# Batch 0 of a Fourier and channel-mix kernel: mirrored rows turned by a copy and added by TensorE, x by plain loads

## The chip, the core and the metric

The kernel runs on one NeuronCore of a Trainium2 chip. Its engines work side by side, each through its own instructions in order: TensorE (PE in the profile, its weight loads PEld), VectorE (DVE), ScalarE (ACT), GpSimd (POOL) and SyncE (SP). TensorE multiplies a stationary operand, loaded first, with a moving one, and writes to PSUM; the others evacuate PSUM to SBUF. Transfers are issued from the queues of SP, ACT and POOL. The metric is the device time of one execution, in microseconds; lower is better.

## The reference

```python
x = randn(8, 3072, 256) * 0.1                       # batch, seq, dim
X = np.fft.fft(np.fft.fft(x, axis=1), axis=2).real   # 2-D Fourier transform, real part
x_prev = X shifted by one row along seq, zero first
xk = mu_k * X + (1 - mu_k) * x_prev
xr = mu_r * X + (1 - mu_r) * x_prev
k = np.maximum(xk @ w_k, 0)                          # 256 -> 1024
v = k * k @ w_v                                      # 1024 -> 256
out = v / (1 + np.exp(-(xr @ w_r)))
```

## The kernel before, in words

The real part of the 2-D transform is a sum of cosines, and row s, column d gives the same as row -s, column -d. So each row of x is added to its mirrored row, read backwards, before anything is multiplied: `fold` (L160 to L175) writes p = x + mirrored x with two VectorE instructions for a piece of rows, one for all columns and one that puts column 0 right. That halves the first stage.

The sequence is taken apart as 3072 = 48 x 64. Batch 0 and 1 lie on 96 partitions (rows 32 apart), the later batches on two groups of 48 (rows 64 apart) at partitions 0 and 64, 112 in all (`parts`, L126). Each batch comes in two halves h, of 9 and 8 row slots. The plain rows (tile xp) come by direct transfers, the mirrored rows (tile xm) by gathers with index tables (`load_m`, L143), all issued on POOL; for batch 0 the first five slots come as 32-bit words through SP (L244), the others are turned to 16 bit on the way.

Three stages follow. Stage a multiplies with a table of cosines and sines over 48 or 96 rows. For batch 0 and the first half of batch 1 that is `a_sum` (L669), which takes p with 208 table columns and adds its two column halves in PSUM; for the second half of batch 1 it is `a_item` (L582), behind `butterfly` (L205), which makes the sum and the difference of the column halves on VectorE. The later batches use the 48-row form `a_half` (L655) or `a_all`, where products of the two groups alternate. Stage d (`d_units`, L695) transforms the columns, stage c (`c_sums`, `c_pairs`) the 64 rows that are left, with the table m_cs. The mix with the previous row follows, and then the feed-forward: `k_piece` (wk products at L912, relu on ScalarE), `square` on VectorE, `v_tile`, `v_part` (wv products, L953 and L965), `r_item` (L939), and `v_out`.

The tables are made on the chip at the start. VectorE writes rows of integers (L324 to L374), TensorE multiplies them to angles (`outer`, L378, into prep and ang_ps), VectorE masks them to one turn, ScalarE takes the sines: w_pm is the 96-row table (L425 to L431), m_cs the last one (L472). w_hh, the 48-row table of the later batches, is picked out of w_pm by TensorE with a selection matrix `order` (L525, L531).

The order of all instructions on every engine is that of the program text (`pin_order`). The preparation of batch 0 is written out by hand, L987 to L1065. From then on a table of steps (`at`, `event`) hangs the work of later batches between the feed-forward pieces, four steps to a chunk of 512 rows. `keep_busy` (L232) issues products of zeros into a PSUM tile that nobody reads; the numbers of them stand in NF.

The few lines at the heart of the part that changes:

```python
mu_rows()                      # L988, ScalarE
...
fold(0, 0, 1, 4)               # L997, VectorE
...
keep_busy(NF[1], fill)         # L1004
a_sum(0, 0, 0)                 # L1005
fold(0, 0, 5, 4)
a_sum(0, 0, 4)
...
fold(0, 1, 0, 4)
a_sum(0, 1, 0, "A")
fold(0, 1, 4, 4)
fold(0, 0, 0, 1)
a_sum(0, 1, 4, "V", 2)
a_sum(0, 1, 6, "A", 2)
```

Of the kernel before, what the change touches and what calls it, by code (L numbers as in the profile page):

```python
# [9 lines left out]
FP32 = mybir.dt.float32  # L10
# [29 lines left out]
def kernel(  # L40
# [18 lines left out]
    NJ, NJ1 = 14, 6  # L59
# [50 lines left out]
    xm_00 = const.tile([96, 514], FP16)  # L110
    xp_00 = const.tile([96, 9, 256], FP16)
    p_sb = [const.tile([112, 256 * (9 - h) + 2], FP16, name=f"p{h}") for h in range(2)]
    xp_32 = const.tile([96, 5, 256], FP32)
    idx_4 = const.tile([96, 2], UINT32)
    idx_8 = const.tile([96, B, 2], UINT32)
    idx_0 = const.tile([96, B], UINT32)
# [9 lines left out]
    def parts(b):  # L126
        return 112 if b > 1 else 96

    def load_p(b, h, q0=0):
        r, n = 9 * h + q0, 9 - h - q0  # L130
        if b > 1:
            for g in range(2):
                src = dataclasses.replace(x[b, 32 * g + r:32 * g + r + 1, :],
                                          ap=[[64 * D, N1], [D, n], [1, D]])
                nc.gpsimd.dma_start(out=xp_t[b, h][64 * g:64 * g + N1, 0:n], in_=src)
            return
        src = dataclasses.replace(x[b, r:r + 1, :], ap=[[32 * D, 96], [D, n], [1, D]])
        nc.gpsimd.dma_start(out=xp_t[b, h][0:96, q0:q0 + n], in_=src)
# [4 lines left out]
    def load_m(b, h, o, n, idx):  # L143
        gather(xm_t[b, h][0:parts(b), XM0 + o:XM0 + o + 256 * n],
               x.rearrange("b (s r) d -> (b s) (r d)", r=n), idx)

    def load_m0(b):
        if b == 0:
            gather(xm_00[:, 1:257], x.rearrange("b s d -> (b s) d"), idx_0[:, 0:1])
        else:  # L150
            load_m(b, 0, 2048, 1, (idx_g0 if b > 1 else idx_0)[:, b:b + 1])

    def load_xh(b, h):
        x_tiles(b, h)
        load_p(b, h)
        if h == 0:
            load_m0(b)
        load_m(b, h, 0, 8, (idx_g8 if b > 1 else idx_8)[:, b, h:h + 1])

    def fold(b, h, q0=0, n=0):  # L160

        n = n or 9 - h
        if (b, h) not in p_t:
            p_t[b, h] = p_sb[h][:, 0:256 * (9 - h)].rearrange("p (q d) -> p q d", d=256)
        k = parts(b)
        p, xp, xm = p_t[b, h][0:k], xp_t[b, h][0:k], xm_t[b, h][0:k]
        o = XM0 + 256 * (8 - h - q0)
        if (b, h, q0) == (0, 0, 0):
            xm, o = xm_00, 1
        if (b, h) == (0, 0) and q0 < 5:  # L170
            xp = xp_32
        V.tensor_tensor(out=p[:, q0:q0 + n], in0=xp[:, q0:q0 + n],  # L172
                        in1=_v(xm, o + 256, [(-256, n), (-1, 256)]), op=ALU.add)
        V.tensor_tensor(out=p[:, q0:q0 + n, 0], in0=xp[:, q0:q0 + n, 0],
                          in1=_v(xm, o, [(-256, n)]), op=ALU.add)  # L175
# [29 lines left out]
    def butterfly(b, h, n=0):  # L205
        n = n or 9 - h
        eo_t[b, h] = eo_pool.tile([112, 9, 2, 128], FP16, name="eo")
        k = parts(b)
        p = p_t[b, h][0:k]
        for e in range(2):  # L210
            V.tensor_tensor(out=eo_t[b, h][0:k, 0:n, e], in0=p[:, 0:n, 0:128],
# [20 lines left out]
    def keep_busy(n, ps, cols=512):  # L232

        for _ in range(n):
# [5 lines left out]
    NF = (8, 4, 1, 3, 0, 0, 0)  # L240
# [3 lines left out]
    nc.sync.dma_start(out=xp_32, in_=dataclasses.replace(x[0, 0:1, :],  # L244
                                                         ap=[[32 * D, 96], [D, 5], [1, D]]))
# [14 lines left out]

    for h in range(2):
        x_tiles(0, h)
    load_p(0, 0, 5)
    for xm in xm_sb:
        V.memset(_v(xm, XM0 + 2048, [(256, 2)]), 0.0)
    V.memset(xm_00[:, 257:258], 0.0)
# [20 lines left out]
    iota(idx_8, pattern=[[S // 8, B], [-1, 2]], base=S // 8 - 1, channel_multiplier=-4)  # L287
    iota(idx_4, pattern=[[-1, 2]], base=S // 4 - 3, channel_multiplier=-8)
    load_m(0, 0, 0, 8, idx_8[:, 0, 0:1])
# [1012 lines left out]
```

## Time and profile before

| | |
|---|---|
| median of 3 runs | 426.06 us (425.98 to 426.39) |
| profiled execution | 426.17 us, span 424.4 us |
| TensorE busy | 418.4 us (99%) |
| VectorE busy | 371.3 us (87%) |
| ScalarE busy | 332.4 us (78%) |
| GpSimd busy | 64.2 us (15%) |

The span is from the first to the last instruction; the execution has 1.8 us around it. A busy TensorE is not one at its peak, since products are pipelined and their ends are modelled. The chain of waits goes back from the last instruction to whatever released each step; the order of time gives each instruction's start and length, where the starts of successive instructions of an engine can lie closer than a length, since they overlap. In rows, "x16" counts instructions, "48*128" is the part of the array that a product uses, and "A<-B" is output and inputs.

### The profile page before, as it was taken

To read this page: it belongs to the slowest core of one execution; us is meant where nothing else is said; L and a number is where in the kernel's file an instruction comes from. 1 tells how busy PE (TensorE), PEld (TensorE's weight loads), DVE (VectorE), ACT (ScalarE), POOL (GpSimd) and SP (SyncE) were. 2 spreads that over 40 slices of the span, in tenths; PEclk is the share of its full clock that TensorE was granted. 3 is DMA by queue.
4 is the path that set the end of the run, shared out by engine and by line. 5 is a ranking of instruction groups with operands and counts; after the bars stand their busy time and mean duration, and the time that the engine had idled before them with its cause. 6 is when DMAs were issued, how large, how long until landed. Compare 5 with 4: busy or idle time off the path is not lost.

```text
span 424.4 us, 9646 instructions
## 1 busy us (share of the span) xinstructions
PE 418.4 (99%) x3974; PEld 294.1 (69%) x3974; DVE 371.3 (87%) x593; ACT 332.4 (78%) x438; POOL 64.2 (15%) x99
## 2 busy tenths in 40 slices
PE   8999999999999999999999999999999999999996
PEld 3767766776677767776767776777777776776765
DVE  8899999999898999989999899989999676977553
ACT  7889886798768986699767996689876997666661
POOL 7478500200060001400041000500000000000000
PEclk9999999999999999999999999999999999999999
DMA  8779962632385223932349232772233232332333
GB/s 171 111 111 195 224 156 57 113 91 64 70 151 147 64 59 62 215 101 51 76 77 220 52 75 59 134 174 55 52 76 72 58 73 52 74 74 51 76 76 99
DMA packets 35104, 42.08 MB, mean 99 GB/s; under 512 B 4114, under 2 KB 31092, under 8 KB 35060
## 3 DMA queue, kind: packets, MB, share of 16 engines
q1 hardware_dynamic: 27488, 25.41, 24.4%
q0 software_dynamic: 7264, 15.80, 21.8%
q8 instruction: 31, 0.51, 0.5%
q10 hardware_dynamic: 308, 0.26, 0.2%
q14 instruction: 13, 0.11, 0.1%
HBM read 32.08 MB, written 25.17 MB: 135 GB/s over the span
## 4 chain that ended last, share of the span: by engine, by line
PE 98%; DVE 1%; issue 0%; POOL 0%; ACT 0%; POOLq 0%
PE psW L912 39%; PE psV L953 37%; PE psW L939 10%; PE psV L965 3%; PE psW L611 3%; PE psW L235 1%; PE psV L611 1%; PE psW L681 1%; PE psW L703 1%; PE psV L378 1%; PE psW L771 0%; PE psW L803 0%; DVE rw L308 0%; PE psV L703 0%; PE psW L663 0%
## 5 line engine op out<-in xcount | busy, mean ns | idle before, releaser
L922 ACT ACTIVATE rl<-psW 128x1024 f16<-128x1024 f32 x192 | 194.3, 1039 | 79.2 <-PE psW L912 75.5
L912 PE MATMUL psW<-x,wk 128*128 128x512 f16 (+1 forms) x776 | 194.4, 377 | 0.3 <-DVE x L1049 0.3
L953 PE MATMUL psV<-wv_sb,k 128*128 128x256 f16 x1424 | 184.2, 273 | 0.0
L953 PEld LDWEIGHTS <-k 128*128 128x128 f16 x1424 | 136.8, 98 | 38.9
L932 DVE TENSOR_TENSOR k<-rl 128x2048 f16<-128x2048 f16 (+1 forms) x100 | 115.5, 1156 | 32.9 <-ACT rl L922 32.8
L912 PEld LDWEIGHTS <-wk 128*128 128x128 f16 x776 | 75.7, 98 | 53.7 <-issue 0.4
L975 DVE SCALAR_TENSOR_TENSOR o<-psV,r 128x512 f32<-128x512 f32 (+1 forms) x97 | 65.7, 680 | 10.0 <-PE psV L953 9.0
L877 DVE TENSOR_TENSOR x<-y,t 128x1536 f16<-128x1536 f16 (+3 forms) x76 | 62.4, 827 | 2.2
L944 ACT ACTIVATE r<-psW 128x1024 f16<-128x1024 f32 x48 | 50.0, 1043 | 0.8 <-PE psW L939 0.8
L939 PE MATMUL psW<-wr,x 128*128 128x256 f16 x384 | 49.8, 273 | 0.0
L939 PEld LDWEIGHTS <-x 128*128 128x128 f16 x384 | 37.5, 98 | 14.1
L574 ACT ACTIVATE a<-psW 128x832 f16<-128x832 f32 (+4 forms) x36 | 29.0, 851 | 0.2 <-PE psW L663 0.2
L574 ACT ACTIVATE g_all<-psW 128x512 f16<-128x512 f32 (+5 forms) x47 | 26.7, 646 | 0.3 <-PE psW L703 0.2
L494 POOL IOTA gate<- 1x1 int32 x7 | 0.8, 121 | 163.4 <-DVE gate L493 163.4
L141 POOL DMA_INDIRECT xm<-in_x_dram,idx_g x18 | 23.3, 1294 | 5.5 <-issue 5.5
L866 DVE TENSOR_SCALAR t<-d,muf_t 128x1536 f16<-128x1536 f16 (+3 forms) x44 | 21.9, 508 | 0.1
L172 DVE TENSOR_TENSOR p<-xp,xm 112x2304 f16<-112x2304 f16 (+6 forms) x19 | 21.6, 1139 | 0.0
L574 ACT ACTIVATE pq<-psW 128x1024 f16<-128x1024 f32 (+1 forms) x21 | 20.4, 1007 | 0.1
L866 DVE TENSOR_SCALAR t<-d,mu_m 128x1536 f16<-128x1536 f16 x32 | 19.6, 611 | 0.0
L854 DVE TENSOR_TENSOR d<-y 128x1664 f16<-128x1664 f16 (+5 forms) x19 | 16.7, 879 | 0.3 <-ACT y L574 0.3
L846 DVE TENSOR_TENSOR y<-pq 128x960 f16<-128x960 f16 (+3 forms) x28 | 15.7, 603 | 0.4
L965 PE MATMUL psV<-wv_sb,k 128*128 128x256 f16 x112 | 14.7, 273 | 0.0
(158 smaller groups left out, 236.3 us busy)
## 6 DMA issues: line engine op xcount, KB each, us to landing
out_dram<-o SPq DMA_DIRECT2D x189, 128.0 KB, 2.4
xp<-in_x_dram POOLq DMA_DIRECT2D x12, 216.0 KB, 5.2
xp<-in_x_dram POOLq DMA_DIRECT2D x13, 192.0 KB, 6.8
xp<-in_x_dram POOLq DMA_DIRECT2D x2, 384.0 KB
wv_sb<-in_moe_w_v_dram POOLq DMA_DIRECT2D x1, 512.0 KB
xp<-in_x_dram SPq DMA_DIRECT2D x1, 480.0 KB, 4.3
xp<-in_x_dram POOLq DMA_DIRECT2D x1, 432.0 KB, 4.9
xm<-in_x_dram,idx_g POOLq DMA_INDIRECT x18, 6.9
```

The costliest lines, as they stand in the source:

```text
L141: nc.gpsimd.indirect_dma_start(dst, None, src, bass.IndirectOffsetOnAxis(ap=idx, axis=0))
L574: nc.scalar.activation(out=out_ap, in_=in_ap, func=AF.Copy)
L866: V.tensor_scalar(out=dst, in0=src, scalar1=mu, scalar2=None, op0=ALU.mult)
L877: V.tensor_tensor(out=_v(x_t[b, j, m], o, [(64 * step, hi - lo), (step, 64)]), in0=y_t[b][:, lo + 3 * m:hi + 3 * m, a], in1=x_t["t", a][:, ...
L912: nc.tensor.matmul(out=st["k", ds][:, 512 * hs + lo:512 * hs + hi], lhsT=wk_sb[m][a][:, 128 * fc:128 * fc + 128], rhs=xk[:, a, 512 * i + l ...
L922: nc.scalar.activation(out=st["rl"][:, 2 * ds:2 * ds + 2], in_=st["k", ds].rearrange("p (f t) -> p f t", f=2), func=AF.Relu, bias=0.0, sca ...
L932: V.tensor_tensor(out=k2_t[c][:, lo:hi], in0=r, in1=r, op=ALU.mult)
L939: nc.tensor.matmul(out=ps[:, 256 * tb:256 * tb + 256], lhsT=x_t[b, 1, m][:, a, 512 * i + 128 * tb: 512 * i + 128 * tb + 128], rhs=wr_sb[m] ...
L944: nc.scalar.activation(out=st["r", c], in_=ps, func=AF.Sigmoid)
L953: nc.tensor.matmul(out=st["v", tb - h][:, 256 * h:256 * h + 256], lhsT=k2_t[c][:, fc, 128 * tb:128 * tb + 128], rhs=wv_sb[:, fc], start=(f ...
L965: nc.tensor.matmul(out=st["v", tb - h][:, 256 * h:256 * h + 256], lhsT=k2_t[c][:, fc, 128 * tb:128 * tb + 128], rhs=wv_sb[:, fc], start=fc ...
L975: V.scalar_tensor_tensor(out=o.rearrange("p a b -> p (a b)")[:, 0:256 * n], in0=st["v", t0][:, 0:256 * n], scalar=16.0, in1=st["r", c][:, ...
```

## The change

Batch 0 takes the form of two groups of 48 rows, as the later batches have it, and is no longer folded by VectorE. The plain rows are multiplied with one table (w_t, version 0) and the mirrored rows with another (version 1), and both products are added in the same PSUM bank (`a_0`, `into`). Since the mirrored rows now come by plain loads in ascending order, `turned_0` turns them: one VectorE copy of 2048 elements read backwards, and a small one for column 0. The zero slot is a row whose own mirror lies in the same tile, and gets a small tile s_00 of rows scaled by the root of 1/2, plain and mirrored (`a_0_self`). The first five slots, which come as 32-bit words, are copied to 16 bit.

The gathers of batch 0 and their index tables go. Its x comes by two transfers on SP and ACT and ten on POOL, each for one group of 48. Two of the mirrored loads fill only part of the rows that are later read; ScalarE writes zeros there first. XM0, the start of the data in tile xm, goes from 257 to 2.

The tables w_t and w_s are made for the 48-row form at once, in nine blocks instead of three, so w_pm, `order` and the three products of `half_tables` go. Of the last table m_cs only 32 of each 64 columns get angles and sines; the others are the same values times +1 or -1 by partition (`m_rest`). Batch 1's first stage becomes `a_sums` and `a_half` in the 48-row form, and its loads those of the later batches. The index patterns of the later batches move from loads_2 to loads.

```diff
-    NJ, NJ1 = 14, 6
+    NJ = 14
-    XM0 = 257
+    XM0 = 2
...
+    def load_0p(h, g, q0, q1):
+        nc.gpsimd.dma_start(out=xp_t[0, h][group(g), q0:q1],
+                            in_=x_rows(0, 32 * g + 9 * h + q0, q1 - q0))
+    def load_0m(h, g):
+        k0 = int((h, g) == (1, 0))
+        nc.gpsimd.dma_start(out=xm_t[0, h][group(g), XM0 + 256 * k0:XM0 + 2048]
+                            .rearrange("p (k d) -> p k d", d=256),
+                            in_=x_rows(0, 56 - 8 * h - 32 * g + k0, 8 - k0))
+    def turned_0(h):
+        p, xm = p_sb[h], xm_t[0, h]
+        V.tensor_copy(out=p[:, 0:2048], in_=_v(xm, XM0 + 2048, [(-1, 2048)]))
+        V.tensor_copy(out=_v(p, 0, [(256, 8)]), in_=_v(xm, XM0 + 1792, [(-256, 8)]))
...
-    NF = (8, 4, 1, 3, 0, 0, 0)
-    nc.sync.dma_start(out=xp_32, in_=dataclasses.replace(x[0, 0:1, :],
-                                                         ap=[[32 * D, 96], [D, 5], [1, D]]))
+    NF = (2, 3, 4, 2, 2, 3, 0, 0, 0)
+    for g, eng in enumerate((nc.sync, nc.scalar)):
+        eng.dma_start(out=xp_32[group(g)], in_=x_rows(0, 32 * g, 5))
...
+    load_0p(0, 0, 5, 9)
+    nc.scalar.activation(out=warm, in_=zeros[:, 0:1], func=AF.Sin, bias=0.0, scale=1.0)
     for h in range(2):
+        lo = 32 - 32 * h
+        nc.scalar.activation(out=xm_t[0, h][lo:64, XM0:XM0 + 2048].bitcast(FP32),
+                             in_=_v(zeros[lo:64], 0, [(0, 16), (1, 128)]).bitcast(FP32),
+                             func=AF.Copy)
...
-    load_m(0, 0, 0, 8, idx_8[:, 0, 0:1])
-    load_p(0, 1)
-    load_m(0, 1, 1024, 4, idx_4[:, 0:1])
-    load_m(0, 1, 0, 4, idx_4[:, 1:2])
+    load_0p(0, 1, 5, 9)
+    for h in range(2):
+        for g in (1, 0):
+            load_0m(h, g)
+    for q0, q1 in ((0, 4), (4, 8)):
+        for g in range(2):
+            load_0p(1, g, q0, q1 - (q1 == 8 and g == 0))
     rows()
-    load_m0(0)
...
-    for n, on, off in ((0, 0.0, TWO_PI / TURN), (1, TWO_PI / TURN, 0.0), (2, 0.0, -math.pi),
-                       (3, -math.pi, 0.0)):
-        nc.scalar.activation(out=sc[:, n:n + 1], in_=g_i, func=AF.Copy, bias=off, scale=on - off)
...
+    for v in range(2):
+        sine(_v(w_t, 2 * WB * v, [(WB, 2), (1, 2), (2, NU)]),
+             _v(u_w, 3 * NU, [(-2 * NU, 2), ((2 * v - 1) * NU, 2), (1, NU)]))
+    sine(_v(w_s, 0, [(2 * NU, 2), (NU, 2), (1, NU)]),
+         _v(u_w, 7 * NU, [(NU, 2), (-2 * NU, 2), (1, NU)]))
+    nc.scalar.activation(out=ang[:, 0, 1:NJ], in_=ang_ps[:, 32:32 * NJ], func=AF.Identity,
+                         bias=ph_c[:, 0:1], scale=float(TURN) / S)
+    for c in range(2):
+        ts(ang[:, c, 0:1], ang_ps[:, 0:32], float(TURN) / S, MUL,
+           ph_c[:, 2 * c + 1:2 * c + 2], ADD)
+    ts(ang[:, 1, 1:NJ], ang_ps[:, 32:32 * NJ], float(TURN) / S, MUL, ph_c[:, 2:3], ADD)
+    ts(ang, ang, TURN - 1, ALU.bitwise_and)
     for c in range(2):
         ts(ueo[:, :, c], _v(prep, P_E, [(64, 2), (1, 64)]), TURN / 256.0, MUL,
            0.75 * (1 - c) * TURN, ADD)
...
+    def m_rest():
+        ts(m_cs[:, 0:2, :, 32:64], m_cs[:, 0:2, :, 0:32], odd_even[:, 0:1], MUL)
...
+    def a_0(h, i0, banks, m):
+        for k in range(2):
+            for i in range(4):
+                for g in range(2):
+                    s = i0 + i
+                    if h and s == 7 and g == 0:
+                        continue
+                    rows = group(g)
+                    if m:
+                        w = p_sb[h][rows, 256 * s + 128 * k:256 * s + 128 * k + 128]
+                    else:
+                        w = xp_t[0, h][rows, s + 1 - h, 128 * k:128 * k + 128]
+                    into(_v(banks[g], 2 * WB * i, [(1, 2 * WB)]), (h, i0, g), w,
+                         _v(w_t[rows], 2 * WB * m, [(WB * k, 2), (1, WB)]))
...
+    m_sine()
     eo_sine()
     eo_rest()
+    for g in range(2):
+        V.tensor_copy(out=xp_00[group(g), 1:5], in_=xp_32[group(g), 1:5])
+    for g in range(2):
+        s, z = s_00[group(g)], xp_32[group(g), 0]
+        ts(s[:, 0], z, math.sqrt(0.5), MUL)
+        ts(s[:, 1, 1:256], _v(z, 255, [(-1, 255)]), math.sqrt(0.5), MUL)
+        ts(s[:, 1, 0:1], z[:, 0:1], math.sqrt(0.5), MUL)
+    mu_rows()
+    b_1 = two(ps_w())
+    a_0(0, 4, b_1, 0)
+    keep_busy(NF[1], fill)
+    m_rest()
+    turned_0(0)
+    a_0(0, 4, b_1, 1)
     nc.scalar.activation(out=warm, in_=zeros[:, 0:1], func=AF.Sigmoid)
-    fold(0, 0, 1, 4)
     mu_ps = ps_v()
...
+    keep_busy(NF[2], fill)
+    b_0 = two(ps_w())
+    a_0(0, 0, b_0, 0)
+    a_0_self(b_0)
+    a_0(0, 0, b_0, 1)
+    for g in range(2):
+        a_0_evac(0, 4, g, b_1[g], "A")
     nc.scalar.activation(out=muf_t, in_=mu_ps[:, 0:6], func=AF.Copy)
     loads()
+    m_neg()
+    keep_busy(NF[3], prep)
+    turned_0(1)
     turn_table()
...
+    for i0, banks in ((0, b_2), (4, b_3)):
+        a_0(1, i0, banks, 1)
+    for g in range(2):
+        a_0_evac(0, 0, g, b_0[g], "AV"[g])
+        evac(_v(a_t[0], 15 + 32 * g, [(64, WB)]), _v(b_0[g], 8 * WB, [(1, WB)]), "AV"[g])
+    for i0, banks in ((0, b_2), (4, b_3)):
+        a_0(1, i0, banks, 0)
+        for g in range(2):
+            a_0_evac(1, i0, g, banks[g], "AV"[g])
     fill = ps_w()
-    keep_busy(NF[3], fill)
+    keep_busy(NF[5], fill)
...
-    at(11, a_sum, 1, 0, 0)
+    event(11, (a_sums, 1, 0, 0), (a_sums, 1, 0, 4))
-    at(12, a_sum, 1, 0, 4)
-    at(13, a_item, 1, 1, 0)
+    event(13, (a_slots_0, 1), (a_half, 1, 1, 0), (a_half, 1, 1, 1))
+    v_behind(12, 14)
-    at(14, a_item, 1, 1, 1)
```

More of the change, by code (lines that the diff above doesn't have):

```diff
@@ new lines, with into @@
+    begun = set()
+    def into(out, bank, lhsT, rhs):
+        nc.tensor.matmul(out=out, lhsT=lhsT, rhs=rhs, start=bank not in begun, stop=False,
+                         skip_group_check=True)
+        begun.add(bank)
+    def a_0(h, i0, banks, m):
+        for k in range(2):
+            for i in range(4):
+                for g in range(2):
[9 more added lines that the diff above has]
+                         _v(w_t[rows], 2 * WB * m, [(WB * k, 2), (1, WB)]))
@@ new lines, in a_0_self, with a_0_evac @@
+    def a_0_self(banks):
+        for m in range(2):
+            for k in range(2):
+                for g in range(2):
+                    rows = group(g)
+                    w = s_00[rows, m, 128 * k:128 * k + 128]
+                    into(_v(banks[g], 8 * WB, [(1, WB)]), (0, 0, g), w,
+                         _v(w_s[rows], WB * m, [(NU * k, 2), (1, NU)]))
+    def a_0_evac(h, i0, g, bank, eng):
+        n = 4 - int((h, i0, g) == (1, 4, 0))
+        evac(_v(a_t[0], 16 * g + 8 * h + i0, [(32, 2 * WB), (1, n)]),
+             _v(bank, 0, [(1, 2 * WB), (2 * WB, n)]), eng)
```

281 lines of the change are left out of this document (96 added, 185 removed).

## The prediction

> **What bounds the kernel now.** I read the page first, for what each engine does over the span.
>
> ```profile
> span 424.4 us, 9646 instructions
> PE 418.4 (99%) x3974; PEld 294.1 (69%) x3974; DVE 371.3 (87%) x593; ACT 332.4 (78%) x438; POOL 64.2 (15%) x99
> ...
> PEclk9999999999999999999999999999999999999999
> ...
> PE 98%; DVE 1%; issue 0%; POOL 0%; ACT 0%; POOLq 0%
> ```
>
> TensorE is the bound for nearly the whole span. So a microsecond counts in two ways here: as TensorE work taken out once the feed-forward products run, or as a shift of the moment at which they begin. The second view is the chain of waits over the first 64 us (start, length, work).
>
> ```profile
> 3.87 2.41 PE psV L378 x6
> 6.28 2.94 PE psW L235 x8
> 9.21 0.53 PE psV L1000 x4
> ...
> 9.79 0.97 PE psW L235 x4
> ...
> 13.13 0.89 PE psV L681 x10
> ...
> 14.66 0.40 PE psV L703 x4
> ...
> 18.25 0.82 PE psW L912 x6
> ...
> 23.57 0.17 PE psW L535 x3
> ...
> 39.49 0.72 PE psW L681 x8
> ```
>
> ```profile
> 45.27 0.32 PE psW L594 x7
> 45.59 0.09 PE psW L591 x2
> ...
> 60.87 0.21 PE psW L663 x16
> ```
>
> The reader should see three things. Batch 0 is prepared until 18.25, where L912, the feed-forward, starts. Its first stage (L681) ends at 14.02, and the second (L703) starts at 14.66. Between, and before, L235 stands in the chain: products of zeros that only keep TensorE running. They also show its speed. Among the eight fillers from 6.28 on, the weight loads follow each other at 0.42:
>
> ```profile
> 6.50 0.15 PEld L235 LDWEIGHTS <-zeros 128*128 128x128 f16 x1 [0.28 <-issue]
> ...
> 6.92 0.15 PEld L235 LDWEIGHTS <-zeros 128*128 128x128 f16 x1 [0.28 <-issue]
> ```
>
> The four fillers at 9.79 take 0.24 each. Eight of them in 2.94 us are then some five slow and three fast ones: TensorE goes over to nearly twice the rate near 8.6, although the page's granted clock reads full throughout. The stretch of wide work before that begins at 3.87 (4.7 us) or, counted from the fillers, at 6.28 (2.3 us).
>
> The third view is the order of time on ScalarE and VectorE.
>
> ```profile
> 0.75 0.41 SPq L244 DMA_DIRECT2D xp<-in_x_dram  x1
> ...
> 2.97 0.46 ACT L356 ACTIVATE sc<-g_i 128x1 f32<-128x1 int32 x4
> ...
> 3.94 0.22 ACT L420 ACTIVATE rw_turn<-ramp 1x4 f16<-1x4 int32 x1
> 4.55 0.62 ACT L428 ACTIVATE w_pm<-u_w,sc 128x104 f16<-128x104 int32 x1 [0.39 <-DVE u_w L308]
> 4.93 0.44 ACT L430 ACTIVATE w_pm<-u_w,sc 128x52 f16<-128x52 int32 x1
> ```
>
> ```profile
> 4.50 0.48 DVE L308 TENSOR_SCALAR ueo<-psW 128x128 int32<-128x128 f32 x2
> 5.01 0.29 DVE L308 TENSOR_SCALAR ueo<-ueo 128x256 int32<-128x256 int32 x1
> ...
> 7.91 0.71 DVE L308 TENSOR_SCALAR rl<-rl 128x1024 int32<-128x1024 int32 x1
> ...
> 8.86 1.22 DVE L172 TENSOR_TENSOR p<-xp,xm 96x1024 f16<-96x1024 f32 x1
> ...
> 13.04 0.16 DVE L174 TENSOR_TENSOR p<-xp,xm 96x1 f16<-96x1 f32 x1
> ```
>
> VectorE finishes the tables at 8.86 and then folds x until 13.2; it is never free in between, and the last L681 waits for the last folds.
>
> **The change, part by part.** Sizes that the kernel does not yet have come from these groups:
>
> ```profile
> L922 ACT ACTIVATE rl<-psW 128x1024 f16<-128x1024 f32 x192 | 194.3, 1039 | 79.2 <-PE psW L912 75.5
> L574 ACT ACTIVATE a<-psV 128x416 f16<-128x416 f32 x1 | 0.6, 552 | 0.0
> L866 DVE TENSOR_SCALAR t<-d,mu_m 128x1536 f16<-128x1536 f16 x32 | 19.6, 611 | 0.0
> L866 DVE TENSOR_SCALAR t<-d,muf_t 128x512 f16<-128x512 f16 x10 | 3.1, 351 | 0.0
> L183 DVE TENSOR_TENSOR t<-p 112x576 f16<-112x576 f16 x10 | 4.2, 457 | 0.0
> L308 DVE TENSOR_SCALAR m_cs<-m_cs 128x896 f16<-128x896 f16 x1 | 0.5, 473 | 0.0
> ```
>
> *ScalarE.* Before, it is through with its small copies at 4.16 (3.94 + 0.22). It gains one x load to issue, about 0.45 us going by SP's row (0.41), and two zero fills of 1024 words, about 0.95 each by the 1024-element group less the overlap; it loses the four sc copies (0.46 busy, 0.4 without the overlap). So it reaches its sines at 4.16 + 0.45 + 1.9 - 0.4 = 6.1, after u_w is ready. Three sines of 104 at 0.38 apiece (4.55 to 4.93) and the angles of 416 (0.55) follow: angles out at about 7.8.
>
> *VectorE.* The new rows of constants cost 0.2 to 0.4 us early and hide behind ScalarE. The mask of the angles now covers both halves at once and therefore waits for ScalarE: 7.8 + 0.6 (896 words, by the 0.71 for 1024) = 8.4. Behind that wait are queued ueo (0.48 and 0.29, which ran earlier before) and all of x's work. So VectorE turns to x at about 9.1, where it was 8.86. Then, in its written order:
> - xp_32 copied to 16 bit, two of 1024. One-source words of four bytes took 0.71; I take 0.65 each with overlap, 1.3. If the type change costs one element at a time (the 1.22 of the fold from 32 bit), 2.4.
> - the six scaled rows s_00: 0.29 for 256 by ueo's row, less for single elements, with overlap 1.0.
> - m_rest, 896 elements: 0.4 by the m_cs row.
> - turned_0(0), a reversed copy of 2048. From 512 to 1536 a one-source instruction of 16 bit grows by 0.26 us, so 2048 would take 0.35 + 0.39 = 0.74, and 0.8 with the little second copy. L183's group holds as many reversed reads from an even address as forward ones, and its mean of 457 ns is that of two elements per step; so reversal as such, and the new even XM0, cost the other batches' folds nothing. The bounds are 0.74 and 2.3 (one element per step, by the 1.22 for 1024); I take 0.8, nearest to the one-source rows.
>
> The first turned copy is out at 9.1 + 1.3 + 1.0 + 0.4 + 0.8 = 12.6. m_neg and turned_0(1) end at 13.8, before TensorE wants them.
>
> [...]
>
> *GpSimd and x.* Six x transfers on its queue become ten:
>
> ```profile
> L138 POOL DMA_DIRECT2D xp<-in_x_dram x4 | 2.5, 621 | 0.9 <-POOLq L1286 0.8
> L141 POOL DMA_INDIRECT xm<-in_x_dram,idx x7 | 7.8, 1113 | 1.7 <-issue 1.5 <-DVE g_i L308 0.2
> 9.72 1.20 POOL L141 DMA_INDIRECT wk<-in_moe_w_k_dram,row_i  x1 [0.30 <-issue]
> DMA to landing us min/median/max: 3.5/5.8/7.7
> ```
>
> Ten at 0.62 against two at 0.62 and four at 1.11 plus gaps: the wk gathers go out near 9.7 as before, and the products that need them start 8.5 us later. Two of the new loads wait for the zero fills, with everything later on the queue behind them; they go out near 4.8 and 5.7, and 5.8 us to land (the median for this tile) makes 10.6 and 11.5, ahead of the turned copies that start at 11.8 and 13.0. I cost this at nothing; without that cover each microsecond late is one on the sum. The index patterns moved into loads() and the dropped zero rows lie on a GpSimd that is idle afterwards: nothing.
>
> *TensorE ahead of 18.25.* Its instructions stay in order, so everything written behind the first turned copy starts after 12.6. With a pair of 48-row products at the price of one (below), sixteen of 104 columns are 8 x 104 columns: 0.37 us at the fast rate, 0.70 at the slow. In order, fast/slow: the turned half of slots 4 to 7, 0.37/0.70; the mu products 0.53 either way; four fillers 0.87/1.71; slots 0 to 3 with their self terms 0.84/1.58; two fillers 0.43/0.85; half 1, turned and plain, 1.42/2.70. Sum 4.46/8.07. The 0.64 from the last product to L703 stays.
>
> Which rate? Before 12.6 TensorE has the table products, two fillers, sixteen products and three fillers, which run out near 9, with a gap where the sines come late; then it stands for about 3.6 us. Wide work without a break before the fast rate was between 2.3 and 4.7 us; I take the middle, 3.5, counted anew from 12.6. So 3.5 us at the slow rate do 3.5 of 8.07, the other 4.6 take 2.3: stage one ends at 18.4 and L703 starts at 19.0, 4.35 later than 14.66. From there to L912 nothing changes.
>
> *TensorE behind 18.25.* Gone: twice 0.72 (L681, its second group alike), twice 0.32 + 0.09 (L594 and L591, likewise), 0.17 (L535): 2.4 us. Added: sixteen 48-row products of 52 columns took 0.21 (L663), 26 ns a pair, where one L594 product of 104 takes 46; so pairs run side by side and sixteen of 104 cost 0.37. Twice that, twice 0.21 and 0.04 for the slots: 1.2. Saved: 1.2, all of it on the chain as long as no evacuation stalls; two wide tiles are now taken within one step, and between 1.2 and 0.7 I keep 1.2 since the chain there has no other engine in it.
>
> The sum: 426.17 (the profiled execution, 1.8 around its span and 0.1 above the median 426.06) + 4.35 - 1.2 = 429.3, and 429.2 on the median.
>
> **The rivals.**
> 1. The fast rate holds over the pause. Then 4.5 instead of 5.8 behind 12.6: L703 at 17.7, +3.1 - 1.2, 427.9. For it: the rate did not drop in any later gap of the chain; against it: none of those gaps is as long as 3.6 us. [...]
> 2. Reversed one-source copies run one element per step: the first turned copy 1.5 later, 430.7. For it: no row of such a copy; against it: L183.
> 3. Faster. The place is the first turned copy: with the fast rate, L703 stands still against the 1.2 saved if that copy is out by 14.66 + 1.2 - 0.64 - 4.46 = 10.8. If ScalarE's fills hide, the type copies take four elements per step, and it is out at 10.0, then 425.3. For it: the folds' 4.3 us leave VectorE; against it: 2.7 us of copies and scalings stand ahead.
> 4. The saving is not there, because pairs of 104 columns do not run side by side or evacuations stall: 0.3 saved in place of 1.2, 430.1. Against it: L663.
>
> **How the numbers follow.** Forecast 0.42, rival 1 0.23, rival 2 0.10, rival 3 0.14, rival 4 0.08, and 0.03 for a draw of 1.2 gained and 1.2 lost. A measurement of this kernel tells about 0.2% (0.9 us) from no change. So faster 0.14, same 0.04, slower 0.82. The range reaches down to the cases near rival 1 with an early copy, 426.8, and up to rival 2 with a slower type copy, 431.5; rival 3 is left out.
>
> **What would show it.** Right: the ACT zero fills of about 1 us each and the mask on VectorE ending after 8; the first 2048-element copy ending near 12.6 in 0.75 us; a hole of over 3 us in TensorE ahead of it; fillers of 0.43 behind it; L703's first product near 19.0; a stretch from there to the end shorter by 1.2. Wrong: TensorE busy without a hole from 9 on, or L703 before 15.9, or the folds of later batches at twice their time.

## The result, and the profile after

The changed kernel takes 438.46 us (437.56 to 438.82), where the kernel before takes 426.13 beside it: a ratio of 1.0285 (95% interval 1.0271 to 1.0298). It is slower, as forecast, but by 12.3 us instead of 3.1, far outside the range of 426.8 to 431.5. The profiled execution took 437.56. The page shows the same picture of a kernel bound by TensorE, with a span 11.4 us longer:

```profile
span 435.8 us, 9900 instructions
...
PE 422.9 (97%) x4098; PEld 296.3 (68%) x4098; DVE 372.5 (85%) x595; ACT 332.7 (76%) x436; POOL 62.5 (14%) x98
...
PEclk9999999999999999999999999999999999999999
...
PE 93%; DVE 5%; issue 0%; ACT 0%; DVEq 0%
```

The chain now has VectorE in it, which was 1% before. Its first part, in order of time (start, length, work):

```profile
14.17 0.65 DVE p L168
...
14.87 0.88 PE psW L655 x13
...
16.73 1.83 PE psW L238 x4
...
20.36 0.98 PE psW L238 x2
...
24.34 1.39 PE psW L238 x3
25.73 0.43 PE psV L699 x4
...
29.56 1.03 PE psW L908 x8
```

L655 is stage one (L681 before), L699 the stage behind it (L703), L908 the first feed-forward product (L912), L238 the fillers. Stage one starts behind the small turned copy (L168) at 14.87, takes until 24.34, and its fillers take 0.46 to 0.49 each throughout: TensorE is slow for all of it, while PEclk reads full. It was slow ahead of its pause too: the sixteen products from 7.08 on take 0.88 and the three fillers at 7.88 take 1.46, so there was no fast rate for the pause to lose. L699 starts at 25.73 instead of 14.66, L908 at 29.56 instead of 18.25. From there to the end it is 435.8 - 29.56 = 406.2, and before 424.4 - 18.25 = 406.2: behind L908 nothing was gained or lost.

VectorE ahead of stage one, in order of time:

```profile
8.06 0.97 DVE L313 TENSOR_SCALAR rl<-psV,ph_c 128x32 int32<-128x32 f32 x3 [1.42 <-ACT rl L436]
9.06 0.64 DVE L313 TENSOR_SCALAR rl<-rl 128x896 int32<-128x896 int32 x1
...
10.33 1.57 DVE L987 CAST xp<-xp 48x1024 f16<-48x1024 f32 x2
11.92 1.13 DVE L313 TENSOR_SCALAR s<-xp 48x256 f16<-48x256 f32 x6
13.08 0.45 DVE L313 TENSOR_SCALAR m_cs<-m_cs,odd_even 128x896 f16<-128x896 f16 x1
13.45 0.69 DVE L167 COPY p<-xm 112x2048 f16<-112x2048 f16 x1
14.17 0.64 DVE L168 COPY p<-xm 112x8 f16<-112x8 f16 x1
```

The reversed copy of 2048 elements takes 0.69 us, as predicted. What is late stands ahead of it: VectorE idles 1.42 us for ScalarE's angles, then computes its own three pieces of them, and only then turns to x.

### The profile page after: what moved, and what is told of

It reads as the page before. It is cut to its first block, busy times and chain, and to the rows that moved or that the text cites. A ratio compares the mean times of both kernels' runs of the same rounds, so it can differ in the third digit from the quotient of the medians.

```text
span 435.8 us, 9900 instructions
## 1 busy us (share of the span) xinstructions
PE 422.9 (97%) x4098; PEld 296.3 (68%) x4098; DVE 372.5 (85%) x595; ACT 332.7 (76%) x436; POOL 62.5 (14%) x98
## 3 DMA queue, kind: packets, MB, share of 16 engines
q0 software_dynamic: 7408, 16.26, 21.6%
## 4 chain that ended last, share of the span: by engine, by line
PE 93%; DVE 5%; issue 0%; ACT 0%; DVEq 0%
PE psW L908 37%; PE psV L949 36%; PE psW L935 9%; PE psW L574 3%; PE psV L961 2%; PE psW L238 1%; PE psW L655 1%; PE psW L699 1%; PE psV L574 1%; DVE x L873 1%; DVE o L971 1%; DVE t L862 1%; DVE rl L313 0%; DVE xp L987 0%; PE psW L626 0%
## 5 line engine op out<-in xcount | busy, mean ns | idle before, releaser
L908 PE MATMUL psW<-x,wk 128*128 128x512 f16 (+1 forms) x776 | 194.1, 377 | 0.3 <-DVE x L1066 0.3
L949 PE MATMUL psV<-wv_sb,k 128*128 128x256 f16 x1424 | 184.2, 273 | 0.0
L908 PEld LDWEIGHTS <-wk 128*128 128x128 f16 x776 | 75.7, 98 | 54.2 <-issue 0.6
L557 ACT ACTIVATE a<-psW 128x936 f16<-128x936 f32 (+6 forms) x38 | 28.5, 803 | 9.2 <-PE psW L655 7.9
L137 POOL DMA_INDIRECT xm<-in_x_dram,idx_g x21 | 26.0, 1240 | 6.5 <-issue 6.1
L176 DVE TENSOR_TENSOR p<-xp,xm 112x2304 f16<-112x2304 f16 (+1 forms) x14 | 18.0, 1285 | 0.6 <-DMA xm<-in_x_dram,idx_g 0.6
L133 POOL DMA_DIRECT2D xp<-in_x_dram x28 | 15.8, 579 | 0.6
```

Of the source, the lines that this page charges most:

```text
L137: nc.gpsimd.indirect_dma_start(dst, None, src, bass.IndirectOffsetOnAxis(ap=idx, axis=0))
L176: V.tensor_tensor(out=p[:, 0:n], in0=xp[:, 0:n], in1=_v(xm, o + 256, [(-256, n), (-1, 256)]), op=ALU.add)
L557: nc.scalar.activation(out=out_ap, in_=in_ap, func=AF.Copy)
L908: nc.tensor.matmul(out=st["k", ds][:, 512 * hs + lo:512 * hs + hi], lhsT=wk_sb[m][a][:, 128 * fc:128 * fc + 128], rhs=xk[:, a, 512 * i + l ...
L949: nc.tensor.matmul(out=st["v", tb - h][:, 256 * h:256 * h + 256], lhsT=k2_t[c][:, fc, 128 * tb:128 * tb + 128], rhs=wv_sb[:, fc], start=(f ...
```

## The experiments

**1. Full-width fillers in the hole.** Is the slow rate the cause?

```diff
-    NF = (2, 3, 4, 2, 2, 3, 0, 0, 0)
+    NF = (2, 18, 4, 2, 2, 3, 0, 0, 0)
```

> The changed kernel with 15 more fillers of 128 rows in TensorE's hole ahead of the first turned copy (NF[1] 3 to 18). Theory A: the hole let TensorE fall to the slow rate, and products of 48 rows do not bring it back. Then all work behind the copy runs at the fast rate, 4.5 us in place of about 10: L699 starts near 20.0 in place of 25.7, the time falls by some 5.5 us to about 432.5. Theory B: the hole alone did it, and products of 48 rows count like others: the same here. Theory C: VectorE's late copies set the end whatever TensorE's rate: 438, unchanged.

Measured: 433.91 (433.87 to 434.27), 4.55 less than the changed kernel. The chain:

```profile
14.87 0.54 PE psW L655 x16
...
15.99 0.98 PE psW L238 x4
...
20.48 1.10 DVE a L555 x2
...
21.72 0.38 PE psV L699 x4
```

Stage one starts at the same 14.87 and its last product ends at 19.91: 5.04 us instead of 9.47. The same sixteen products take 0.54 instead of 0.88, four fillers 0.98 instead of 1.83. So the slow rate alone cost 4.4 us of stage one, and 4.0 at L699; Theory C falls. What is left, the late copy and the tail (1.8 us from the last product to L699, with two evacuations of VectorE in a row), holds L699 at 21.72, later than the 20.0 of Theories A and B.

**2. The same hole filled with 48-row products.** Does TensorE stay slow because of the pause, or because of the narrow products?

```diff
+    def keep_busy_48(n, ps):
+        for _ in range(n):
+            for g in range(2):
+                z = zeros[group(g)]
+                nc.tensor.matmul(out=ps[:, 512 * g:512 * g + 512], lhsT=z,
+                                 rhs=_v(z, 0, [(0, 4), (1, P)]), start=True, stop=True)
...
+    keep_busy_48(15, fill)
     m_rest()
```

> The changed kernel with the same hole filled by 15 pairs of 48-row products of zeros, 512 columns each. Theory A: TensorE is busy without a hole and is slow all the same, L699 near 25 to 26, about 438. Theory B: as with fillers of 128 rows, L699 near 20, about 432.5. Theory C: 438 in both.

Measured: 434.61 (433.91 to 435.08). TensorE in order of time:

```profile
7.07 0.88 PE L662 MATMUL psW<-w_t,xp 48*128 48x104 f16 x16 [0.47 <-ACT w_t L435]
7.88 1.46 PE L238 MATMUL psW<-zeros 128*128 128x512 f16 x3
9.28 6.58 PE L245 MATMUL psW<-zeros 48*128 48x512 f16 x30
...
17.90 0.54 PE L662 MATMUL psW<-w_t,xp 48*128 48x104 f16 x16
```

Thirty 48-row products of 512 columns in 6.58 us are 0.44 a pair: the two of a pair do run side by side, but at the slow rate to their end (their weight loads come by twos, 0.43 apart from 9.68 to 15.23, as those of single full-width fillers do in run 1 while these are slow). Sixteen products of stage one then take 0.54. So narrow products do bring the fast rate back, but in this execution only after some 8.8 us of work without a break (7.07 to 15.86). The theory that they don't count at all falls. In run 1, with full-width fillers in the same place, TensorE was fast from 10.79, 3.7 us after the same start.

**3. No fillers behind the first turned copy.** Do they pay for themselves?

```diff
-    NF = (2, 3, 4, 2, 2, 3, 0, 0, 0)
+    NF = (2, 3, 0, 0, 2, 0, 0, 0, 0)
```

> The changed kernel without the nine fillers behind the first turned copy (four, two, three). Nine at 0.46 are 4.1 us of TensorE's chain. Theory A and B: the rate stays slow and lasts into the next stages, which lose up to 1.5 us: L699 near 21.6, total 434 to 436. Theory C: no change, 438.

Measured: 436.95 (435.54 to 437.03), above the 434 to 436 of Theories A and B, with L699 at 22.23 instead of 21.6. TensorE is still slow in the first wk products, where the changed kernel takes 1.03 for as many:

```profile
22.23 0.58 PE psV L699 x4
...
26.81 1.70 PE psW L908 x8
```

L908 starts 2.75 us earlier than in the changed kernel, and only 1.5 of these reach the end, since the rate comes back later. The fillers are work on the path, and with them TensorE was fast earlier (by 26.98 in the changed kernel, where five products of L767 take 0.34; the same five take 0.50 here, and the first wk products are slow up to 28.35). Here the first weighs more.

**4. Batch 1's first stage in the old order.** Why is nothing saved behind L908? Each wide tile is hung on its own step again, the 48-row form stays.

```diff
-    event(11, (a_sums, 1, 0, 0), (a_sums, 1, 0, 4))
+    at(11, a_sums, 1, 0, 0)
...
+    at(12, a_sums, 1, 0, 4)
...
-    event(13, (a_slots_0, 1), (a_half, 1, 1, 0), (a_half, 1, 1, 1))
-    v_behind(12, 14)
+    at(13, a_late, 1, 0)
...
+    at(14, a_late, 1, 1)
```

> The changed kernel with batch 1's first stage hung at the old places: each half of it ahead of the wv products of steps 11 to 14, not behind them. Theory: those products now wait for a PSUM bank that VectorE has yet to read, and nothing covers the wait; in the old place the first stage covers it, and the 1.2 us of shorter products come out: 437.4 by about -1.0. Rival: the loss there is VectorE's, which waits 0.6 us for the mirrored rows of batch 1: no change.

Measured: 436.53 (435.74 to 438.47). From the first wk product (27.47) to the end of the span (434.0) it is 406.5: no gain, as the rival said. The lower total was made ahead of it, where nothing was edited: in this execution the fillers at 20.20 are already fast (two in 0.55), in the changed kernel's they are slow (0.98 at 20.36). The moment at which TensorE becomes fast differs from execution to execution. In the stretch itself VectorE now waits for the mirrored rows:

```profile
51.02 1.23 DVE L176 TENSOR_TENSOR p<-xp,xm 112x2048 f16<-112x2048 f16 x1 [0.88 <-DMA xm<-in_x_dram,idx_g]
```

**5. VectorE's order ahead of the first turned copy**, on top of run 1.

```diff
+    (ueo: two scalings and a mask)
+    for g in range(2):
+        V.tensor_copy(out=xp_00[group(g), 1:5], in_=xp_32[group(g), 1:5])
     for c in range(2):
         ts(ang[:, c, 0:1], ang_ps[:, 0:32], float(TURN) / S, MUL,
            ph_c[:, 2 * c + 1:2 * c + 2], ADD)
...
     ts(ang, ang, TURN - 1, ALU.bitwise_and)
...
-    m_rest()
     turned_0(0)
+    (the scaled rows s_00)
+    m_rest()
```

The lines in brackets stand for blocks that move unchanged. ScalarE does the sine of w_eo and the rows of mu ahead of the sine of m_cs, and NF[1] is 11.

> Edit: on top of the variant with full-width fillers in the hole, VectorE does the angles w_eo needs and the 16-bit copies of x before the pieces of the last table's angles (for which it waited 1.42 us on ScalarE), and the scaled rows s_00 and m_rest come behind the first turned copy instead of ahead of it; ScalarE does the sine of w_eo ahead of the one of m_cs; fillers in the hole 11 instead of 18. The whole output is computed. Theory A (the lateness of the first turned copy passes to the end one to one once the rate is fast): the copy is out at 6.6 + 0.7 + 1.6 + 1.0 + 0.6 + 0.9 = 11.6 instead of 14.82, L699 at 18.5, time 433.9 - 3.2 = 430.7. Theory B (behind it another engine takes over: ScalarE's sine of 896, table load and evacuations of stage one): L699 not before 20, time 432 or more.

Measured: 431.64 (431.03 to 432.41).

```profile
11.00 0.31 DVE p L168
...
16.97 1.10 DVE a L557 x2
...
18.20 0.38 PE psV L701 x4
```

The copy is out at 11.31, 3.5 us earlier, and the next stage (L701 here) starts 3.5 us earlier, at 18.20. Theory A holds for the start. The time falls by 2.3 only, to 431.64 instead of 430.7: from the first wk product (21.77) to the end it is 407.8 in this execution against 406.9 in run 1. In this kernel's chain a transfer of batch 1's mirrored rows appears, which was not there in run 1; whether that is the 0.9 us was not tested.

**6 and 7. Less VectorE work behind L908, in both kernels.** The fold of batch 1's second half is left out, in run 1's kernel and in the kernel before.

```diff
+        if (b, h) == (1, 1):
+            return
         p, xp, xm = p_t[b, h], xp_t[b, h], xm_t[b, h]
```

> Edit: the variant with 18 full-width fillers in the hole, and the fold of batch 1's second half left out (two VectorE instructions, 1.5 us together); p keeps batch 0's rows there, so batch 1's output isn't the reference's; all else is computed. To be read beside the same omission in the kernel before. Theory A (in steps 8 to 14 VectorE is the bound, so the shorter TensorE work of the change cannot show): the omission takes 1.0 to 1.5 us off 433.9, to 432.4 to 432.9, and more here than in the kernel before, by up to the 1.2 us of TensorE work saved. Theory B (the new products take as long as those they replaced, VectorE is not the bound): under 0.4 us off.

> Edit: the kernel before, with the fold of batch 1's second half left out in the same way (batch 1's output isn't the reference's; all else is computed). Theory A (VectorE the bound of both kernels there, the kernel before with 1.2 us more TensorE work in the same stretch): 0.2 to 1.0 us off 426.1, less than the same omission takes off the changed kernel. Theory B: the same amount off in both, or nothing in both.

Measured: 433.91 in the changed kernel, which took 433.91 in run 1, and 426.26 in the kernel before, which took 426.46 beside it. 1.5 us of VectorE left out, and nothing gained in either. My theory in this form falls: VectorE is not the bound of the whole stretch. The rows of the changed kernel say where it is one. They show VectorE without a pause from an output product to the next, and TensorE waiting for the latter, all ahead of the fold that was left out (the fold at 44.34 is that of batch 1's first half):

```profile
41.65 1.29 DVE o L971 x2
...
44.34 1.28 DVE p L176
...
50.44 0.61 DVE o L971
...
51.10 1.19 PE psV L961 x8
```

**8. Everything early.** No zero fills (the short mirrored loads read 64 rows), mirrored loads ahead of half of the plain ones, both turned copies ahead of the angles, plain products in the hole.

```diff
-        nc.scalar.activation(out=xm_t[0, h][lo:64, XM0:XM0 + 2048].bitcast(FP32),
-                             in_=_v(zeros[lo:64], 0, [(0, 16), (1, 128)]).bitcast(FP32),
-                             func=AF.Copy)
...
-    load_0p(0, 1, 5, 9)
-    for h in range(2):
-        for g in (1, 0):
-            load_0m(h, g)
+    load_0m(0, 1)
+    load_0m(0, 0)
+    load_0p(0, 1, 5, 9)
+    load_0m(1, 1)
+    load_0m(1, 0)
```

> Edit: the changed kernel with its start put in another order, the whole output computed: no zero fills on ScalarE (the two short mirrored loads read 64 rows instead), those loads earlier on the queue, the angles of w_eo before the long ones on TensorE, VectorE in the order u_w, ueo, 16-bit copies, both turned copies, then the rest of the angles and the scaled rows; TensorE multiplies plain rows in the hole, half 1 after slots 4 to 7 and 0 to 3; Sigmoid's table loaded after stage c's first evacuation. Theory A (the start decides): first turned copy out near 9, L699 near 14, time 425 to 426.5, the level of the kernel before. Theory B (TensorE still runs slow behind a start of mostly 48-row products, or x is not there by 8): L699 at 16 to 18, time 427.5 to 430.

Measured: 436.05 (434.38 to 437.74), far outside what either theory gave.

```profile
9.13 0.87 PE L648 MATMUL psW<-w_t,xp 48*128 48x104 f16 x15 [2.75 <-DMA xp<-in_x_dram]
...
11.19 0.69 DVE L167 COPY p<-xm 112x2048 f16<-112x2048 f16 x1 [1.83 <-DMA xm<-in_x_dram]
...
26.72 0.40 PE L760 MATMUL psV<-m_cs,g_all 64*128 64x128 f16 x8 [1.23 <-ACT g_all L550]
```

The first turned copy ends at 9.36, but the plain rows that were moved back arrive only at 9.1 and hold TensorE for 2.75 us; it comes out of that pause slow (0.87) and stays slow through stage one. The turned products of that stage start 1.8 us earlier than in run 1 and the first wk product 1.75 later, 1.23 of it by Sigmoid's table (its load takes 1.28 from 25.09), which I had put where TensorE waits for ScalarE. The second turned copy waits for its rows until 11.19: the transfers bound this start from below.

**9 and 10. Batch 1's order again, with TensorE fast; then its loads earlier.** Run 9 is run 1 with the edit of run 4. Run 10 adds:

```diff
+        load_xh(1, 1)
         for a in range(2):
             gather(wk_sb[1][a], moe_w_k, row_i[:, 2 + a:3 + a])
-        load_xh(1, 1)
```

> Edit: the variant with 18 full-width fillers in the hole (433.91), with batch 1's first-stage products put back to one wide tile per step, as in the kernel before; the 48-row form stays. The whole output is computed. This repeats the test of the order with a TensorE that is fast from the start of stage one, so that the moment of waking can't cover it. Theory A (two wide tiles taken in one step hold the PSUM banks and stop the wk products): 0.5 to 0.8 us less, 433.1 to 433.4. Theory B (the order doesn't matter, the loads of batch 1 arrive too late): 433.7 to 434.1, with a wait of VectorE's fold for the mirrored rows in the trace.

> Edit: the one before, and batch 1's second half is loaded ahead of the second pair of wk gathers on GpSimd's queue instead of behind it (3 us earlier). The whole output is computed. Theory B (the mirrored rows of batch 1 come too late for its fold, 0.88 us of waiting in the trace of the old order): a further 0.4 to 0.6 us less than the run without it, and the fold (1,1) starts without a wait for a DMA. Rival: the time stays, since the wk gathers now come later, or since VectorE then waits elsewhere.

Measured: 433.65 (433.34 to 434.19) and 433.58 (433.35 to 434.01). Both lie 0.3 below run 1's 433.91, but the kernel before, run beside each, lay 0.2 lower as well, and the ratios to it are 1.0172 and 1.0176 against run 1's 1.0173: neither the order nor the earlier load gives anything that can be told. Run 9's time falls between the two theories, and the wait of the fold for the mirrored rows that Theory B gave is not in its trace (the fold starts at 48.52 without one), so run 10 had no such wait to remove. Neither is by itself what ate the saving.

**11. The start laid anew**, from run 8: loads back in the old order, eight full-width fillers between the angles and the first products, then stage one with two fillers in all; the last angles ahead of the first turned copy; Sigmoid's table right behind the sines; batch 1 as in run 10.

```diff
...
-    NF = (1, 3, 2, 2, 0, 3, 0, 0, 0)
+    NF = (8, 0, 0, 2, 0, 3, 0, 0, 0)
...
```

> Edit: the start in another order than in the run with everything early (436.05), the whole output computed. Eight full-width fillers without a break from the angles to the first plain products, then plain and turned products of slots 4 to 7, 0 to 3 and half 1 in turn with two fillers in all between them; VectorE: ueo, 16-bit copies, the last angles, first turned copy, scaled rows, two evacuations, second turned copy; Sigmoid's table right behind the sines; batch 1 as in the run with the early load. Theory A (TensorE kept on full-width products wakes ahead of 10, the rest is set by when x lands): first turned copy out at 9.3, L699's products at 15, time 425.8 to 427.5. Theory B (the second turned copy or ScalarE is later than that): L699 at 16 to 17.5, time 427.5 to 430.

Measured: 427.30 (426.92 to 430.39), within Theory A's range, and a ratio of 1.0040 (1.0015 to 1.0065) to the kernel before.

```profile
9.77 0.19 DVE L168 COPY p<-xm 112x8 f16<-112x8 f16 x1
...
15.70 0.38 PE L698 MATMUL psV<-w_eo,a 128*128 128x128 f16 x4 [0.34 <-DVE a L548]
```

The copy is out at 9.96 and the second stage starts at 15.70, 0.7 later than Theory A gave and 1.0 after the kernel before: 11.2 of the 12.3 us lost are back with the 48-row form, the mirrored rows by copy and the plain loads all kept.

**12. The output product first.** Does the wait of TensorE on VectorE's o decide the stretch behind L908?

```diff
-    OUT_FIRST = (12, 20, 28, 36, 38, 40, *(24 * t - 48 + k for t in range(3, B) for k in (28, 32, 36)))
+    OUT_FIRST = (10, 12, 20, 28, 36, 38, 40, *(24 * t - 48 + k for t in range(3, B) for k in (28, 32, 36)))
```

> Edit: one number on top of the run with the start relaid (427.30): 10 is added to OUT_FIRST, so that in step 10 VectorE does the output product of batch 0 (o) ahead of the mix of slots 16 to 24 instead of behind it; the whole output is computed. In the traces of the changed kernel and of all its variants VectorE works 9.5 us without a break up to that o, and TensorE's next wv products wait for it. Theory A (in that one stretch VectorE, not TensorE, sets the pace, so that a shorter TensorE earns nothing ahead of it): the wv products behind the first sums of batch 1 start without a wait on VectorE, the stretch from the first wk product to the end is 0.2 to 0.4 us shorter than 406.15, time 426.9 to 427.1. Theory B (the wait only moves, to the fold or the squares that now come later): stretch and time unchanged within 0.1.

Measured: 429.50 (427.29 to 430.77), and in the profile 406.3 from the first wk product to the end: Theory A's 0.2 to 0.4 are not there. The wait is gone all the same; the chain of this stretch is TensorE alone but for 0.22:

```profile
43.67 0.47 PE psW L639 x16
44.14 0.98 PE psV L960 x8
...
45.34 0.22 issue
```

The kernel before, in the same place:

```profile
39.49 0.72 PE psW L681 x8
40.20 0.88 PE psV L965 x8
...
41.94 0.71 PE psW L681 x8
42.66 0.87 PE psV L965 x8
```

The sums take 0.47 instead of 0.72, but the wv products behind them 0.98 instead of 0.88: each return from 48-row to full-width products costs 0.1 in these rows. In this order there are four such returns, behind the two sums (the second at 46.86, 0.98 as well) and the two other products.

What raised the total against run 11 lies in the start, which has the same program. Its eight fillers, in run 11:

```profile
5.54 2.66 PE L238 MATMUL psW<-zeros 128*128 128x512 f16 x8
```

and in run 12, with the rows behind them and the line of the granted clock, a digit for each fortieth of the span:

```profile
5.54 3.62 PE L238 MATMUL psW<-zeros 128*128 128x512 f16 x8
...
12.89 0.61 PE L238 MATMUL psW<-zeros 128*128 128x512 f16 x2
14.01 0.88 PE L654 MATMUL psW<-w_t,p 48*128 48x104 f16 x16 [0.51 <-DVE p L168]
...
18.58 1.49 PE L698 MATMUL psW<-w_eo,a 128*128 128x128 f16 x12
...
PEclk9699999999999999999999999999999999999999
```

In run 11 TensorE became fast among these fillers (the last three weight loads, from 7.18, take 0.53 in all), in run 12 only near 10 (0.88 for the sixteen products at 9.09, 0.54 for those at 10.22). There the fillers at 12.89 are fast, the products at 14.01 slow again, and so is all up to the second stage (1.49 for the twelve products that take 0.83 at the fast rate). This fall is in the clock: the trace grants 0.50 from 13.4 to 20.1, and 1.00 everywhere else, also ahead of 10, where the products were just as slow. A fast TensorE fell back in a start made mostly of 48-row products, with pauses of 0.3 to 0.5 us between them. Run 11's profiled execution has such pauses too, one of them 1.34 long, and kept the rate; why one start holds and the other doesn't was not tested.

The clock of the other executions is on record as a mean. The three longest of run 11 (429.99 to 430.39) had 0.990 to 0.992, the other seven (426.92 to 427.51) 0.998 to 1.000; the profiled one of run 12 (430.69) had 0.992. So the same start lost the rate in some executions of both runs. Those of run 12 with 0.997 and more took 427.29 to 428.08: putting the output product first gained nothing there either.

## Why the prediction was wrong

The sign was right, and so was the mechanism of the start: behind the first turned copy a slow TensorE, L699 late, no wait on batch 0's transfers. The saving behind L908 was not there. Five terms of the sum were mis-sized, all to the same side (predicted, measured in the profiled execution):

| step | predicted | measured | error |
|---|---|---|---|
| first turned copy out | 12.6 | 14.82 | +2.2 |
| stage one, from there to its last product | 5.8 | 9.5 | +3.7 |
| last product to L699 | 0.64 | 1.39 | +0.75 |
| L699 to L908 | 3.6 | 3.8 | +0.2 |
| saved behind L908 | 1.2 | -0.1 | +1.3 |

Together 8.2, and 429.3 + 8.2 = 437.5, the profiled 437.56; the median lies 0.9 higher. (In the sum itself, the fast part of stage one comes to 2.4 by its own terms, not 2.3, a slip of 0.1.)

*The rate of TensorE* is the step that failed most. I took 3.5 us of work as the time to wake, the middle of what the kernel before showed for full-width fillers, which makes the slow rate cost 1.3 of the 5.8 us. It cost 4.4 here (run 1), because the fast rate did not come back before the end of stage one. Runs 2 and 12 show why the number did not carry over: it was measured on products that fill the array, while in run 2 TensorE stayed slow through 6.6 us of 48-row products without a pause, and in run 12 it lost the rate among them. Nor is it one number: with the same program the moment of waking moved by some 3 us between the executions of runs 11 and 12. Rival 1, that the fast rate holds over the pause, had nothing to hold, since TensorE was slow ahead of it as well; where it was fast, in run 1, the rate did last over a pause of 1.54 us. A part of the term was also the plain price: at the fast rate stage one takes 5.04 (run 1) against my 4.46. Sixteen products that follow sixteen others do start 0.36 apart, as I had it (17.02 and 17.38 in run 1), but where the kind of product changes the chain takes 0.1 to 0.2 more than I added: sixteen 0.54 instead of 0.37, four fillers 0.98 instead of 0.87.

*The first turned copy.* ScalarE was as predicted (angles out at 8.0, fills 2.14), the reversed copy too (0.69 for 0.74), so rival 2 is out. The step that failed is "So VectorE turns to x at about 9.1": I let only the mask wait for ScalarE, while the three pieces of the angles, 0.97 us, stand in VectorE's order behind the same wait. Of the rest, the type copies took 1.57 for 1.3 and the small copy of 8 elements 0.64, with GpSimd issuing a transfer from 13.84 on for 0.97 us; the second such copy, at 15.70 with no transfer issued beside it, takes 0.19. Run 5 puts the price on the term: 3.5 us earlier there, 3.5 earlier at L699.

*The tail.* "The 0.64 from the last product to L703 stays" failed twice. That 0.64 is three fillers at the fast rate, in the kernel before:

```profile
14.02 0.65 PE psW L235 x3
```

In the changed kernel the same three are slow and take the 1.39 of its chain. And the last two tiles of half 1 are now finished nearly together, so that VectorE evacuates both groups' second halves one after the other: 1.10 in runs 1 and 5, where TensorE is fast and this is the chain. In the changed kernel the second of them ends at 25.32, so L699 could have started little earlier than its 25.73 even with fast fillers.

*The saving behind L908.* Rival 4 named the outcome. One of its two grounds was wrong: pairs do run side by side, as run 2 shows. The other, that evacuations stall, is in the rows: o reads its operand out of PSUM, and TensorE waits for it. I priced the new products by L663's 0.21 and left out the row behind it, a wv product that takes 0.98. The changed kernel takes two wide tiles at a time, so it has two returns: its chain saves 1.43 - 0.84 on the sums (32 products in 0.84), 0.82 - 0.56 on the others, 0.17 by L535 and loses twice 0.1, which leaves 0.8. That goes in the wait for o: TensorE idles 0.45 ahead of the wv products at 51.10, and these take 1.19 instead of 0.87. The step that failed is "the chain there has no other engine in it": true of the kernel before, but in the changed kernel VectorE is without a pause in that very place.

With the same two tiles at a time, run 1 loses 0.7 more in this stretch. Its chain goes from the sums to ScalarE, which starts to evacuate them into a at 49.88, when the wv products behind them (48.80 to 49.85) are done too, and from there to the next wk products at 50.80:

```profile
48.03 1.83 PE psW L640 x32
49.88 0.88 ACT a L557
```

A like pair of rows is in the chains of runs 2, 3, 5, 6 and 8, whose stretches from the first wk product to the end take 407.0 to 408.3; run 9 (407.1) has ScalarE in its chain some microseconds later; the changed kernel and runs 4, 10, 11 and 12 (406.1 to 406.5) don't have it. From the 32 products with which stage c of batch 1 begins (L803 at 56.26 before, L799 at 67.61 after) to the end, every kernel takes 368.1 to 368.2, so all of these losses lie in the 38 to 40 us ahead of that.

In the old order there are four returns and some 0.4 is left, which 0.88 of waiting for rows (run 4) or the waits and longer products around it (run 12) take. Runs 4, 6, 9 and 12 each removed one candidate, and none brought the saving out: run 12 took the wait for o away and gained nothing. So these waits are read from the rows, and no run here shows that removing them gives the saving back.

Rival 3, faster, needed the copy out by 10.8 with a fast TensorE. Run 11 has it out at 9.96 and still starts its second stage at 15.70: the second turned copy waits behind evacuations, and half 1 can't start before 12.97. So the condition I gave for it was too weak. No version here beats the kernel before.

Not settled: what decides when TensorE goes over to the fast rate, why ScalarE's evacuation holds the wk products in run 1 and not in the changed kernel, which has the same order there, and whether the old order would show its 0.4 with all waits gone at once.

## What to carry to other kernels

A waking time read from full-width products did not hold for 48-row ones here, and moved by 3 us between executions of one program: where a start is turned into 48-row products with waits between them, price TensorE at half rate until the rows show it fast (in run 1 the full-width fillers were slow from 7.88 to 10.79, in run 5 those at 7.87 were fast at once: eleven in 2.55), or put fillers of full width into the pauses, as run 1 did (4.55 us less). Where one profiled execution is all there is, compare its granted clock with that of the other executions. When a wait is found for one instruction, check every instruction that reads the same producer, since on an engine in order they all stand behind it (here 0.97 us of pieces behind 1.42 of waiting). And price narrow products together with the change back to wide ones (0.1 us each here), which shows in the row behind them and not in their own.

## What the runs showed of the hardware

The clock that the profile's page calls granted read full all through the changed kernel; only the lengths of equal products (0.46 for a filler here, 0.24 in the kernel before) told the two rates apart. In run 12 it shows the rate being lost (0.50 from 13.4 to 20.1), but not the equally slow products ahead of 10. So a full reading at the start of a span does not show that TensorE is fast. A VectorE copy of 8 elements took 0.64 us while GpSimd issued a transfer, and ended with the issue: 13.84 + 0.97 = 14.81. In run 5 the copy at 11.00 took 0.30 and ended at 11.30, as a gather's issue did (9.94 + 1.34 = 11.28); in the changed kernel, with none beside it, it took 0.19 (15.70). Not every issue does this: in run 11 the copy at 9.77 took 0.19 in the middle of a gather's (9.39 to 10.67). Just ahead of the first of these, a GpSimd memset took 0.58 us beside the 2048-element copy, against 0.10 in run 5 without a copy beside it. Why one issue goes with a longer copy and another doesn't was not shown.

```profile
13.60 0.58 POOL L473 MEMSET m_cs<- 64x2 f16 x1 [1.57 <-DVE m_cs L313]
13.84 0.97 POOL L479 DMA_DIRECT2D wv_sb<-in_moe_w_v_dram  x1
```
